# Six more half chunks of attention values as three float32r products, in an attention and mixture-of-experts kernel on one core

## The chip, the core and the metric

The kernel runs on one core of a Trainium2 chip. The core has TensorE (PE, with its weight loads shown as PEld), VectorE (DVE), ScalarE (ACT), GpSimd (POOL) and SyncE (SP), and 16 DMA engines. The metric is the device time of one execution in microseconds, the median of three runs.

## What is computed

```python
def _attn_ref(q, k, v, tau):                      # B, N, C = 4, 5056, 256
    qn = q / (np.linalg.norm(q, axis=1, keepdims=True) + 1e-06)
    kn = k / (np.linalg.norm(k, axis=1, keepdims=True) + 1e-06)
    s = kn.transpose(0, 2, 1) @ qn / tau          # 256 x 256 for each batch
    a = softmax(s, axis=-1)
    return v @ a                                  # 4 x 5056 x 256

def _moe_ref(x, w_gate, w1, w2):                  # 20224 tokens, 8 experts, F = 1024
    logits = x @ w_gate
    # greedy: largest logits first, each token to one expert, 2528 tokens to an expert
    for e in range(E):
        h = np.maximum(x[mask] @ w1[e], 0.0)
        out[mask] = h @ w2[e]
```

All inputs and the output are float32.

## The kernel before

**Stages.** First the scores of the four batches are made from q and k, with as much of the other work as fits beside the loads. Then comes the stage that the change touches, called the value stage here: the product v @ a for the batches 1 to 3 (what is left of it), whose rows are stored to x_d in HBM, while VectorE finds the tokens of expert 0 (route 0). Then the eight experts follow, each with five chunks of 512 tokens: tokens are gathered from x_d by indirect transfers (L1284), layer 1 (L1498) and layer 2 (L1549) run on TensorE, and the rows of the output are scattered (L1567). The routes of the experts 1 to 7 run on VectorE beside the layers of the experts before.

**The value stage.** The rows of v are tiled in chunks of 1024 rows, five to a batch, and a chunk in two halves of four tiles of 128 rows. A half chunk is done in one of two ways. *Plain* (x_tiles, L267): eight float32 matmuls, two for each tile. *Cloven* (x_tiles_cut, L583): v and a are each split in a high half (rounded to float32r) and a low half (what is left), and each float32 product becomes three float32r products, high by high, high by low and low by high: 24 matmuls. The string TURNS gives the order, F for a plain half chunk and C for a cloven one; before there are 12 F and 10 C, and eight plain pairs of tiles (four half chunks) follow. Both ways put two tiles in one PSUM tile px, which ScalarE copies to xs (L271, L587); a store to x_d of each half chunk is issued from ScalarE's queue (L277).

**The split of a half chunk** is done by cleave(): ScalarE writes minus the rounded values to the low part (L568), a transfer issued by GpSimd adds the raw values from HBM to it (L569, an accumulating transfer of 512 KB), and ScalarE writes the rounded values to the high part (L571). The split halves live in buffers named by PLACES (ub0, ub1, ua0 to ua2, vr); BEHIND says after how many F and C turns a buffer may be taken again.

**Route 0** is a search in eight rounds. A round is: VectorE compares (ge, L730), TensorE counts (20 small matmuls into the bank pc, L695, then one with Ex, L708), VectorE reads the counts (mxs, L715) and ScalarE copies them out of the bank (eq, L723). There is one bank pc: the counting of the next round writes it again and has to wait for the copy of the round before. Two lists of tokens are then made (L915 and L935 on TensorE, L953 on ScalarE, L969 on VectorE), the first with the four tiles of the first gather.

**What sets the order.** Each engine works its instructions in the order in which the program lists them. That order is made by a planner (class Order): tick() adds what TensorE does to the planner's time o.pe, and hook() puts VectorE's and ScalarE's pieces of the streams where the planner's time for them has come. advance() decides in the same way about the tokens of a chunk to come: if they landed early enough by the planner's time (`left(*todo[0]) > MOVE_LAT + 4000`), stage() flips them by VectorE and two DMAs by way of HBM (via, xT); if not, turn() transposes them on TensorE with eight matmuls (L1451), four at a time.

```python
        if todo and todo[0] not in BY_PE and landed.get(todo[0], 1e12) <= o.pe and left(*todo[0]) > MOVE_LAT + 4000:
            stage(*todo[0], 0)
            staging.append([todo[0], 1, 0, 1e12])
```

**The weights of expert 0** are loaded when its number is known (L1243) and split in eight pieces by split_piece() (ScalarE L1262, VectorE L1265), one piece after a pair of tiles or half a cloven half chunk; FREED says after how many C turns the buffers ua0 and ua1 are free for that. Layer 1 of expert 0 needs the first four pieces and the transposed tokens of its first chunk (xH by ScalarE, xL by VectorE).

Of the kernel before, what the change touches and what calls it, by code (L numbers as in the profile page):

```python
# [21 lines left out]
E, F = 8, 1024  # L22
# [84 lines left out]
def attention_moe(ctx: ExitStack, tc: tile.TileContext, q, k, vt, tau, wg, w1t, w2t, tabs, out):  # L107
# [449 lines left out]

    cloven = [(b, c, h) for b, c in CLOVEN for h in range(0, T, TH)]
    v_cut = []

    def cleave():
        b, c, h = cloven[len(v_cut)]
        home = PLACES[len(v_cut)]
        y = (vp.tile([128, 2048], F32, name="vr", bufs=BUFS_V) if home == "vr" else
             ffw.tile([128, 2048], F32, name=home)).bitcast(F32R)
# [5 lines left out]
        S.activation(y[:, 0], raw, AF.Copy)  # L571
        v_cut.append(y.rearrange("p z k (t n) -> p z k t n", t=TH))

    def x_tiles_cut(k, t, xs, tick):
        b = cloven[k][0]
# [1011 lines left out]
    with tc.manual_schedule():  # L1587
# [4 lines left out]
        def first_w():  # L1592
            load_w(0, 0)
            load_w(0, 1)
            cut_w[0] = [o.pe + LOAD_LAT] + list(SPLIT)
# [4 lines left out]
        def tend():  # L1600
            settle()
            if cut_w[0] and o.pe > cut_w[0][0] and len(cut_w[0]) > 1 and past.count("C") >= FREED[cut_w[0][1][0]]:
                split_piece(0, *cut_w[0].pop(1))
# [12 lines left out]
        place = halve_a(2)  # L1616
        for _ in range(3):
            cleave()
        place()
        P.memset(ge[:, :, NT:J], 0.0)  # L1620
        for kind in TURNS:
            while len(v_cut) < len(cloven) and len(v_cut) <= len(past) + 1:
                want_ = BEHIND.get(len(v_cut), "")
                if any(past.count(x) < want_.count(x) for x in set(want_)):
# [5 lines left out]
            else:  # L1630
                k = past.count("C")
                b, c, h = cloven[k]
# [9 lines left out]
        actx.close()  # L1642
        px_at[1] = False
# [159 lines left out]
```

## Time and profile before

| | us |
|---|---|
| median of three runs | 1211.24 (1211.0 to 1211.59) |
| time of the profiled execution | 1216.66 |
| its span, first to last instruction | 1214.6 |
| value stage in it, TensorE's first L267 of batch 3 to the first L1498 | 219.6 to 314.3 |

| engine | busy us of the span | share |
|---|---|---|
| PE | 1192.0 | 98% |
| PEld | 1069.0 | 88% |
| DVE | 893.6 | 74% |
| ACT | 579.6 | 48% |
| POOL | 411.2 | 34% |

The granted clock of TensorE is 0.998 of full speed over the span. Matmuls are pipelined, so the end of one row and the start of the next overlap; what a row of matmuls takes is read from its start to the start of the next row. A float32 matmul of the program stands as two in the trace's counts.

### The profile page before, as it was taken

The numbers are of one execution on the slowest core, as the hardware profiler recorded it, in microseconds if no ns is written. First come the engines' busy times: TensorE is split into PE (matmuls) and PEld (weight loads), VectorE is DVE, ScalarE is ACT, GpSimd is POOL, SyncE is SP. The second block draws the span as 40 slices with busy tenths as digits, with TensorE's granted clock in tenths as the row PEclk, the third lists the DMA queues.
The fourth block names the chain that finished last, engine by engine and source line by source line (L and its number), as shares of the span: only waits on it lengthen the run. The fifth ranks groups of instructions, "written<-read, shape, count | busy, mean of one in ns | idle before, by whom it ended". The sixth has DMA issues, their size and how long they took to land.

```text
span 1214.6 us, 22477 instructions
## 1 busy us (share of the span) xinstructions
PE 1192.0 (98%) x8201; PEld 1069.0 (88%) x8201; DVE 893.6 (74%) x2497; ACT 579.6 (48%) x1316; POOL 411.2 (34%) x659
## 2 busy tenths in 40 slices
PE   7999999999999999999999999999999999999998
PEld 6889877798889889999998999988888898898897
DVE  7788686778788888989888888798786555555541
ACT  6666644655343444444354454354445644344431
POOL 1000001110342543354434444444444444444422
PEclk9999999999999999999999999999999999999999
DMA  8998996785322413313422243243234233433310
GB/s 311 361 393 313 365 357 214 182 236 219 107 70 90 146 58 110 140 56 114 143 87 83 79 151 114 83 143 121 82 118 152 87 116 122 140 102 98 105 66 34
DMA packets 70542, 184.27 MB, mean 152 GB/s; under 512 B 11168, under 2 KB 34592, under 8 KB 65824
## 3 DMA queue, kind: packets, MB, share of 16 engines
q1 hardware_dynamic: 39808, 97.54, 22.4%
q0 software_dynamic: 20656, 63.72, 17.4%
q10 hardware_dynamic: 9968, 21.59, 4.6%
q8 instruction: 64, 1.05, 0.4%
q14 instruction: 46, 0.38, 0.1%
HBM read 123.04 MB, written 59.51 MB: 150 GB/s over the span
## 4 chain that ended last, share of the span: by engine, by line
PE 82%; DVE 7%; issue 5%; POOL 2%; DMA 2%; ACT 1%; SPq 0%; POOLq 0%; DVEq 0%; ACTq 0%
PE py L1549 30%; PE ph L1498 30%; PE s L345 8%; PE px L267 5%; PE pc L695 3%; PE px L583 2%; PE px L308 2%; PE px L461 1%; POOL out_dram L1567 1%; DMA ua<-in_q_dram 1%; DVE acc_q L355 1%; DVE hL L1507 1%; DVE acc_k L355 1%; DVE nf L412 1%; PE pi L935 1%
## 5 line engine op out<-in xcount | busy, mean ns | idle before, releaser
L1549 PE MATMUL py<-ua,hH 128*128 128x256 f32 (+2 forms) x1928 | 432.0, 312 | 0.0
L1498 PE MATMUL ph<-xH,ua 128*128 128x512 f32 (+1 forms) x1280 | 392.4, 380 | 1.2 <-DVE hL L1507 1.0
L1549 PE MATMUL py<-ua,hL 128*128 128x256 f32 (+1 forms) x1280 | 339.0, 275 | 0.0
L1549 PEld LDWEIGHTS py<-ua,hH 128*128 128x128 f32 (+1 forms) x1928 | 311.9, 190 | 14.0
L1502 ACT ACTIVATE hH<-ph 128x512 fp32r<-128x512 f32 (+1 forms) x320 | 189.8, 593 | 199.6 <-PE ph L1498 188.3
L1498 PEld LDWEIGHTS ph<-xH,ua 128*128 128x128 f32 x1280 | 240.8, 189 | 32.5 <-DVE hL L1507 2.9
L1507 DVE SCALAR_TENSOR_TENSOR hL<-ph,hH 128x512 fp32r<-128x512 f32 (+1 forms) x320 | 216.1, 677 | 58.8 <-ACT hH L1502 48.0
L1567 POOL DMA_INDIRECT out_dram<-y,idx x160 | 165.6, 1035 | 264.2 <-DVE y L1565 115.3
L1549 PEld LDWEIGHTS py<-ua,hL 128*128 128x128 f32 (+1 forms) x1280 | 243.4, 190 | 4.2
L1498 PE MATMUL ph<-xL,ua 128*128 128x512 f32 (+1 forms) x640 | 242.2, 378 | 0.2 <-DVE xL L1457 0.2
L1284 POOL DMA_INDIRECT xg<-x_d,src x160 | 164.0, 1025 | 91.0 <-issue 54.8
L1561 ACT ACTIVATE y<-py 128x256 f32<-128x256 f32 (+1 forms) x160 | 61.5, 384 | 251.4 <-PE py L1549 191.3
L345 PE MATMUL s<-ua 128*128 128x256 f32 (+1 forms) x640 | 144.4, 384 | 6.4 <-DMA ua<-in_q_dram 6.4
L345 PEld LDWEIGHTS s<-ua 128*128 128x128 f32 (+1 forms) x640 | 121.1, 192 | 26.1 <-DMA ua<-in_q_dram 6.4
L1498 PEld LDWEIGHTS ph<-xL,ua 128*128 128x128 f32 x640 | 121.1, 189 | 14.3 <-DVE xL L1457 0.8
L1565 DVE TENSOR_TENSOR y<-py,y 128x256 f32<-128x256 f32 x79 | 33.4, 423 | 98.3 <-ACT y L1561 95.6
L354 ACT ACTIVATE sq<-ua 128x1024 f32<-128x1024 f32 (+1 forms) x80 | 76.6, 970 | 54.3 <-DMA ua<-in_k_dram 18.2
L1295 POOL COPY spacer<-hH 1x1 f32<-1x1 f32 x114 | 26.1, 229 | 180.9 <-ACT hH L1502 173.0
L375 POOL TENSOR_SCALAR ny<-ny 128x4 f32<-128x4 f32 x4 | 2.0, 506 | 181.1 <-ACT ny L374 181.1
L1383 DVE TENSOR_TENSOR xL<-xT,xH 128x256 fp32r<-128x256 f32 x136 | 51.9, 426 | 6.1 <-ACT xH L1379 6.1
L1379 ACT ACTIVATE xH<-xT 128x256 fp32r<-128x256 f32 x136 | 54.1, 458 | 4.8 <-DMA xT<-via 4.8
L355 DVE TENSOR_TENSOR acc_k<-acc_k,sq 128x1024 f32<-128x1024 f32 (+2 forms) x40 | 44.3, 1113 | 11.2 <-ACT sq L354 10.4
(343 smaller groups left out, 1468.0 us busy)
## 6 DMA issues: line engine op xcount, KB each, us to landing
x_d<-xs ACTq DMA_DIRECT2D x40, 512.0 KB
ua<-in_k_dram SPq DMA_DIRECT2D x35, 512.0 KB
ua<-in_q_dram SPq DMA_DIRECT2D x35, 512.0 KB
via<-xs SPq DMA_DIRECT2D x34, 512.0 KB
xT<-via SPq DMA_DIRECT2D x136, 128.0 KB
vr<-in_vt_dram SPq DMA_DIRECT2D x14, 1024.0 KB
ua<-in_vt_dram SPq DMA_DIRECT2D x4, 1024.0 KB
ua<-in_vt_dram POOLq DMA_DIRECT2D x5, 512.0 KB
```

The source lines that it names most:

```text
L267: mm = PE.matmul(px[:, i * C:i * C + width], lhsT=vs[b, c][:, kb, t + i, :], rhs=a_f[b][:, kb, 0:width], start=(kb == 0), stop=(kb == 1))
L345: newest[0] = PE.matmul(sb[:, ib * C:(ib + 1) * C], lhsT=kt[:np_, t, ib * 128:(ib + 1) * 128], rhs=qt[:np_, t, :], start=(first and t == 0 ...
L354: S.activation(sq[:n, t0:t1], t_[:n, t0:t1], AF.Square)
L355: V.tensor_tensor(acc[:n, t0:t1], acc[:n, t0:t1], sq[:n, t0:t1], op=OP.add)
L1284: P.indirect_dma_start(out=xg[:n, i, :], out_offset=None, in_=rows, in_offset=bass.IndirectOffsetOnAxis(ap=routed[p]["src", col][:n, col:c ...
L1379: S.activation(hi[:, a], rows[:, a], AF.Copy)
L1498: PE.matmul(ph[:, 0:nt], lhsT=l[:, w], rhs=in_turn(x_, kb, nt).rearrange("p a m -> p m a"), start=(i == 0), stop=(i == 5))
L1502: S.activation(hH[:, fb, 0:nt], ph[:, 0:nt], AF.Relu)
L1507: V.scalar_tensor_tensor(hL[:, fb, 0:nt], ph[:, 0:nt], 0.0, hH[:, fb, 0:nt].bitcast(F32), op0=OP.max, op1=OP.subtract)
L1549: PE.matmul(to, lhsT=l[:, fb, tk], rhs=r, start=(fb == 0 and k_ == 0), stop=(fb == 7 and at_end), skip_group_check=twice)
L1561: S.activation(y[:n], py[:n, C:2 * C] if twice else one, AF.Copy)
L1567: sd = P.indirect_dma_start(out=out, out_offset=bass.IndirectOffsetOnAxis(ap=routed[p]["idx", col][:n, col:col + 1], axis=0), in_=y[:n], i ...
```

## The change

Six half chunks of batch 1 go from the plain to the cloven way: CLOVEN now names 16 half chunks, PLAIN five chunks, and TURNS has 6 F and 16 C. The eight plain pairs at the end remain. The a of batch 1 is split by halve_a_1() (two copies by ScalarE, one subtraction by VectorE). Three of the six half chunks (BY_DVE) get their low half by one subtraction on VectorE in place of ScalarE's first copy and the transfer; the other three as before. So there are 13 accumulating transfers of 512 KB in place of 10. One more buffer (own) is added, the rules for taking a buffer again are renewed (AFTER), cleave() may run one turn further ahead, and the weights of expert 0 are split only after all 16 C turns.

```diff
-PLAIN = ((3, 0), (1, 2), (3, 1), (3, 2), (1, 3), (1, 4), (3, 3), (3, 4))
-CLOVEN = ((2, 4), (2, 0), (2, 1), (2, 2), (2, 3))
-TURNS = "FFCFCFCFCFCFCFCFCFFCFC"
-PLACES = ("ub0", "ub1", "ua0", "ua1", "ub0", "ub1", "vr", "ua0", "ua1", "ua2")
-BEHIND = {3: "FF", 4: "C", 5: "CC", 6: "FFFF", 7: "CCC", 8: "CCCC", 9: "FFFFFF"}
-FREED = (9, 10)
+PLAIN = ((3, 0), (3, 1), (3, 2), (3, 3), (3, 4))
+CLOVEN = ((2, 4, 0), (1, 2, 0), (2, 4, 4), (2, 0, 0), (1, 2, 4), (2, 0, 4), (2, 1, 0), (1, 3, 0), (2, 1, 4), (2, 2, 0), (1, 3, 4),
+          (2, 2, 4), (2, 3, 0), (1, 4, 0), (2, 3, 4), (1, 4, 4))
+BY_DVE = (1, 4, 7)
+TURNS = "FFCCFCCCCFCCCCFCCCFCCC"
+PLACES = ("ub0", "ub1", "own", "ua0", "ua1", "ub0", "ub1", "own", "ua0", "ua1", "vr", "ub0", "own", "ua0", "vr", "ua1")
+AFTER = {4: (2, 0), 5: (0, 1), 6: (0, 2), 7: (0, 3), 8: (0, 4), 9: (0, 5), 11: (0, 6), 12: (0, 8), 13: (0, 9), 15: (0, 10)}
+FREED = 16
...
+    def halve_a_1():
+        a = a_f[1][:, :, 0:C].rearrange("p k (m a) -> p k m a", a=2)
+        h = apart(apool.tile([128, 2, GW], F32R, name="a0"))[:, :, :, 0:128]
+        S.activation(h.rearrange("p a k m -> p k m a"), a, AF.Copy)
+
+        def low():
+            less = x_rows()[:, 0:2].rearrange("p k (m a) -> p k m a", a=2)
+            V.tensor_tensor(less, a, h.rearrange("p a k m -> p k m a").bitcast(F32), op=OP.subtract)
+            lo = apart(apool.tile([128, 2, GW], F32R, name="a1"))[:, :, :, 0:128]
+            S.activation(lo.rearrange("p a k m -> p k m a"), less, AF.Copy)
+            a_two[1] = [h, lo]
...
-        S.activation(y[:, 1], raw, AF.Copy, scale=-1.0)
-        P.dma_start(out=y[:, 1], in_=vt[b, c].rearrange("p (k n) -> p k n", k=2)[:, :, h * 128:(h + TH) * 128],
-                    accum_op=OP.add)
+        if k_ not in BY_DVE:
+            S.activation(y[:, 1], raw, AF.Copy, scale=-1.0)
+            P.dma_start(out=y[:, 1], in_=vt[b, c].rearrange("p (k n) -> p k n", k=2)[:, :, h * 128:(h + TH) * 128],
+                        accum_op=OP.add)
         S.activation(y[:, 0], raw, AF.Copy)
+        if k_ in BY_DVE:
+            unit[0] += 1
+            o.post(o.pe + CUT_LAT, 1150,
+                   lambda: V.tensor_tensor(y[:, 1], raw, y[:, 0].bitcast(F32), op=OP.subtract), unit[0])
...
-            while len(v_cut) < len(cloven) and len(v_cut) <= len(past) + 1:
-                want_ = BEHIND.get(len(v_cut), "")
-                if any(past.count(x) < want_.count(x) for x in set(want_)):
+            while len(v_cut) < len(CLOVEN) and len(v_cut) <= len(past) + 2:
+                f_, c_ = AFTER.get(len(v_cut), (0, 0))
+                if past.count("F") < f_ or past.count("C") < c_:
                     break
                 cleave()
```

The lines of the changed kernel are shifted: L270 and L274 are the plain matmul and its copy, L612 and L616 the cloven ones, L590, L591 and L593 the copy, transfer and copy of cleave(), L724 and L737 the counting, L752 the copy of the counts, L1480 the transposes, L1527 and L1578 the two layers.

**ScalarE in the value stage, before.** From the copy of the counts of the second round (eq<-pc) to that of the third; xs<-px are the copies of the products, ua and vr the split halves.

```order
L723 ACTIVATE eq<-pc 128x120
L587 ACTIVATE xs<-px 128x512 x2
L277 DMA x_d<-xs 128x1024
L568 ACTIVATE ua_2085<-vr 128x1024
L571 ACTIVATE ua_2085<-vr 128x1024
L271 ACTIVATE xs<-px 128x512
L723 ACTIVATE eq<-pc 128x120
```

Between the two copies of counts stands one split. **The same place in the change**, again from the copy of the counts of the second round to that of the third:

```order
L752 ACTIVATE eq<-pc 128x120
L616 ACTIVATE xs<-px 128x512
L280 DMA x_d<-xs 128x1024
L590 ACTIVATE ua_2140<-vr 128x1024
L593 ACTIVATE ua_2140<-vr 128x1024
L590 ACTIVATE vr<-vr 128x1024
L593 ACTIVATE vr<-vr 128x1024
L616 ACTIVATE xs<-px 128x512 x2
L280 DMA x_d<-xs 128x1024
L590 ACTIVATE ub_2210<-vr 128x1024
L593 ACTIVATE ub_2210<-vr 128x1024
L752 ACTIVATE eq<-pc 128x120
```

Now three splits (six copies of 128x1024) and three copies of products stand ahead of the copy of the counts.

**TensorE at the same place, before**, from the third round's count with Ex (L708) to the next use of the bank pc (the small matmuls with ge, L695, 20 of them):

```order
L267 MATMUL px<-a_last,ua_1571 128x256 x3
L708 MATMUL pc<-Ex,ones_q 128x128
L267 MATMUL px<-a_last,ua_1571 128x256 x3
L583 MATMUL px<-a_two,ua_1851 128x256 x14
L695 LDWEIGHTS ge
L695 MATMUL pc<-oh,ge 128x64
```

**And in the change:**

```order
L612 MATMUL px<-a_two,ub_1897 128x256 x7
L270 MATMUL px<-a_last,ua_1571 128x256
L737 MATMUL pc<-Ex,ones_q 128x128
L270 MATMUL px<-a_last,ua_1571 128x256 x7
L724 LDWEIGHTS ge
L724 MATMUL pc<-oh,ge 128x64
```

The cloven half chunk ub_1897 is the one during which ScalarE is at the splits shown above; the 17 matmuls of it ahead of these rows have the 20 small matmuls of the third round behind them.

**TensorE in layer 2 of expert 0's fourth chunk, in the change**, where the first chunk of expert 1 is transposed:

```order
L1578 MATMUL py<-ua_3060,hH 128x256
L1578 MATMUL py<-ua_3059,hL 128x256
L1480 MATMUL pt<-identr,xg 128x128 x4
L1578 MATMUL py<-ua_3059,hH 128x256
L1578 MATMUL py<-ua_3060,hH 128x256
```

Before, no transposes stand here: this chunk goes by way of HBM. Over the program TensorE has 72 transposes in place of 48; the first chunk of expert 1, the second of expert 2 and the first of expert 3 are new among them, and SyncE's queue has 31 transfers to via in place of 34, and 124 from it in place of 136.

## Rows read from the trace of the kernel before

**Rows 1.** The page, busy time, share of the span and instructions.

```profile
PE 1192.0 (98%) x8201; PEld 1069.0 (88%) x8201; DVE 893.6 (74%) x2497; ACT 579.6 (48%) x1316; POOL 411.2 (34%) x659
```

**Rows 2.** Windows of the value stage: us, then busy us (instructions) by engine.

```profile
219.60:297.50 77.90, 77.14 (x626) 70.76 (x625) 65.04 (x227) 43.63 (x81) 9.91 (x10) 1.00 0.76 222
297.50:314.30 16.80, 15.58 (x96) 13.39 (x95) 13.50 (x45) 10.63 (x30) 4.34 (x4) 1.00 0.43 158
```

**Rows 3.** Timeline of TensorE: start, length, line, out<-in, count, idle before.

```profile
219.62 7.17 PE L267 MATMUL px<-a_last,ua 128*128 128x256 f32 x32
226.44 3.03 PE L583 MATMUL px<-a_two,ub 128*128 128x256 f32 x24
...
240.68 0.23 PE L708 MATMUL pc<-Ex,ones_q 128*128 128x128 f32 x1
240.74 2.56 PE L583 MATMUL px<-a_two,ua 128*128 128x256 f32 x21
243.14 1.03 PE L267 MATMUL px<-a_last,ua 128*128 128x256 f32 x4
244.00 0.75 PE L695 MATMUL pc<-oh,ge 128*128 128x64 bf16 x20
244.59 1.54 PE L267 MATMUL px<-a_last,ua 128*128 128x256 f32 x6
...
281.80 0.44 PE L935 MATMUL pi<-E__97,G 128*128 128x162 bf16 x4
...
290.84 0.59 PE L935 MATMUL pi<-E__97,G 128*128 128x162 bf16 x6
291.27 0.64 PE L267 MATMUL px<-a,vr 128*128 128x256 f32 x2
...
297.54 5.34 PE L267 MATMUL px<-a_last,vr 128*128 128x256 f32 x24
...
309.46 0.62 PE L1451 MATMUL pt<-identr,xg 128*128 128x128 f32 x2 [1.16 <-DMA xg<-x_d,src]
```

**Rows 4.** Timeline of TensorE in layer 2 of expert 0, around four transposes.

```profile
334.52 0.39 PE L1549 MATMUL py<-ua,hH 128*128 128x256 f32 x2
...
334.85 0.39 PE L1549 MATMUL py<-ua,hH 128*128 128x256 f32 x2
...
335.19 0.45 PE L1451 MATMUL pt<-identr,xg 128*128 128x128 f32 x4
...
335.88 0.39 PE L1549 MATMUL py<-ua,hH 128*128 128x256 f32 x2
```

**Rows 5.** Timeline of ScalarE in the value stage.

```profile
243.46 0.25 ACT L723 ACTIVATE eq<-pc 128x120 f32<-128x120 f32 x1
243.61 1.07 ACT L587 ACTIVATE xs<-px 128x512 f32<-128x512 f32 x2
244.72 0.33 ACTq L277 DMA_DIRECT2D x_d<-xs  x1
245.09 1.06 ACT L568 ACTIVATE ua<-vr 128x1024 fp32r<-128x1024 f32 x1 [0.40 <-ACT xs L587]
...
247.00 0.58 ACT L271 ACTIVATE xs<-px 128x512 f32<-128x512 f32 x1
...
298.15 0.60 ACT L587 ACTIVATE xs<-px 128x512 f32<-128x512 f32 x1
```

**Rows 6.** Timeline of GpSimd: two issues of accumulating transfers, and the first gather.

```profile
238.94 1.09 POOL L569 DMA_DIRECT2D ub<-in_vt_dram  x1 [5.28 <-ACT ub L568]
...
302.40 0.95 POOL L1284 DMA_INDIRECT xg<-x_d,src  x1 [20.91 <-ACT xs L271]
```

**Rows 7.** DMA from 245 to 265 us: busy tenths of 40 slices of 0.5 us.

```profile
DMA  8689999999899999999989999999997999999999
```

**Rows 8.** Timeline of VectorE: the end of the first list, and a subtraction of 128x512.

```profile
285.74 0.16 DVE L1010 SCALAR_TENSOR_TENSOR src<-k,w__2659 128x4 int32<-128x4 int32 x1
...
313.04 0.69 DVE L1457 TENSOR_TENSOR xL<-pt,xH 128x512 fp32r<-128x512 f32 x1 [1.30 <-ACT xH L1454]
```

**Rows 9.** Groups by line and form: a two-operand pass of 128x1024 on VectorE, mean ns.

```profile
L355 DVE TENSOR_TENSOR acc_q<-acc_q,sq 128x1024 f32<-128x1024 f32 x32 | 39.1, 1221 | 2.5 <-ACT sq L354 2.3
```

More of the change, by code (lines that the diff above doesn't have):

```diff
@@ L69 @@
 HOMES = {(1, 0): "ub", (1, 1): "ub", (2, 4): "ua", (3, 0): "ua", (3, 1): "ua", (3, 2): "ua", (3, 3): "late", (3, 4): "late"}
-PLAIN = ((3, 0), (1, 2), (3, 1), (3, 2), (1, 3), (1, 4), (3, 3), (3, 4))
-CLOVEN = ((2, 4), (2, 0), (2, 1), (2, 2), (2, 3))
-TURNS = "FFCFCFCFCFCFCFCFCFFCFC"
-PLACES = ("ub0", "ub1", "ua0", "ua1", "ub0", "ub1", "vr", "ua0", "ua1", "ua2")
-BEHIND = {3: "FF", 4: "C", 5: "CC", 6: "FFFF", 7: "CCC", 8: "CCCC", 9: "FFFFFF"}
-FREED = (9, 10)
+PLAIN = ((3, 0), (3, 1), (3, 2), (3, 3), (3, 4))
[6 more added lines that the diff above has]
+FREED = 16
+CUT_LAT = 3000
 CUT = (4, 4, 4, 4, 4)
@@ L556, in halve_a @@
         return place
-    cloven = [(b, c, h) for b, c in CLOVEN for h in range(0, T, TH)]
+    def halve_a_1():
[9 more added lines that the diff above has]
+        unit[0] += 1
+        o.post(o.pe + CUT_LAT, 600, low, unit[0])
+    cctx = ExitStack()
+    own = cctx.enter_context(tc.tile_pool(name="own", bufs=1))
     v_cut = []
+    lows_of = {}
     def cleave():
-        b, c, h = cloven[len(v_cut)]
-        home = PLACES[len(v_cut)]
-        y = (vp.tile([128, 2048], F32, name="vr", bufs=BUFS_V) if home == "vr" else
+        k_ = len(v_cut)
+        b, c, h = CLOVEN[k_]
+        home = PLACES[k_]
+        y = (own.tile([128, 2048], F32, name="own") if home == "own" else
+             vp.tile([128, 2048], F32, name="vr", bufs=BUFS_V) if home == "vr" else
              ffw.tile([128, 2048], F32, name=home)).bitcast(F32R)
@@ L567, in cleave @@
         raw = vs[b, c][:, :, h:h + TH].rearrange("p k t n -> p k (t n)")
-        S.activation(y[:, 1], raw, AF.Copy, scale=-1.0)
-        P.dma_start(out=y[:, 1], in_=vt[b, c].rearrange("p (k n) -> p k n", k=2)[:, :, h * 128:(h + TH) * 128],
-                    accum_op=OP.add)
+        if k_ not in BY_DVE:
+            S.activation(y[:, 1], raw, AF.Copy, scale=-1.0)
+            P.dma_start(out=y[:, 1], in_=vt[b, c].rearrange("p (k n) -> p k n", k=2)[:, :, h * 128:(h + TH) * 128],
+                        accum_op=OP.add)
         S.activation(y[:, 0], raw, AF.Copy)
+        if k_ in BY_DVE:
+            unit[0] += 1
+            o.post(o.pe + CUT_LAT, 1150,
+                   lambda: V.tensor_tensor(y[:, 1], raw, y[:, 0].bitcast(F32), op=OP.subtract), unit[0])
+        lows_of[k_] = unit[0]
         v_cut.append(y.rearrange("p z k (t n) -> p z k t n", t=TH))
     def x_tiles_cut(k, t, xs, tick):
-        b = cloven[k][0]
+        b = CLOVEN[k][0]
+        if b == 1:
+            o.flush(lows_of[k])
         px = next_px()
@@ L1592, in first_w @@
         def first_w():
+            assert past.count("C") >= 12
             load_w(0, 0)
@@ L1601, in tend @@
             settle()
-            if cut_w[0] and o.pe > cut_w[0][0] and len(cut_w[0]) > 1 and past.count("C") >= FREED[cut_w[0][1][0]]:
+            if cut_w[0] and o.pe > cut_w[0][0] and len(cut_w[0]) > 1 and past.count("C") >= FREED:
                 split_piece(0, *cut_w[0].pop(1))
@@ L1616, in attention_moe @@
         place = halve_a(2)
+        halve_a_1()
         for _ in range(3):
@@ L1631, in attention_moe @@
                 k = past.count("C")
-                b, c, h = cloven[k]
+                b, c, h = CLOVEN[k]
                 xs = x_rows()
@@ L1642, in attention_moe @@
         actx.close()
+        cctx.close()
         px_at[1] = False
```

## The prediction

> **What bounds the kernel now.** I read the busy times first [rows 1]: TensorE is busy in 1192.0 of 1214.6 us, 98%, the next engine, VectorE, in 74%. So a change counts here by what it takes from TensorE's work and by the waits that it makes on TensorE. Then the windows of the value stage [rows 2]: TensorE is busy in 77.14 of 77.9 us and 15.58 of 16.8 us, so there are only about 2 us of idle time in the stage, 1.16 us of them in one wait, for the first gathered tokens at 309.46 [rows 3]. VectorE is busy in 65.0 of the 77.9 us and ScalarE in 43.6; neither bounds the stage by its sum, but both work in the order listed, and TensorE can wait for a single copy that stands behind others. Third, the timelines, for the prices and the places.
>
> **TensorE's work in the six half chunks.** Two plain half chunks run from 219.62 to 226.44 [rows 3], 3.41 us each, or 0.426 us for each of eight matmuls. Of a cloven half chunk 21 matmuls run from 240.74 to 243.14, 0.114 us each, so 24 take 2.74 us. Six half chunks save 6 x 0.67 = **4.0 us**, all of it on the path, because TensorE is busy throughout.
>
> **TensorE's work that comes back.** The order shows 72 transposes on TensorE in place of 48: three chunks of experts 1 to 3 no longer reach the planner's limit for the way by HBM, because the routes of the experts now fall later against the layers. Their price is in layer 2 of expert 0 [rows 4]: a group of three matmuls follows the one before by 0.33 us (334.52 to 334.85); the two groups around four transposes take 1.03 us (334.85 to 335.88) in place of 0.68. So four transposes cost 0.35 us, and the six new fours **2.1 us**. I take the same price where they stand in layer 1. Nothing hides them, since TensorE has no idle time there. What they free on VectorE, SyncE and the DMA queues was not waited for.
>
> **New waits for ScalarE.** The bank pc is counted into again only after ScalarE has copied the last counts. Before, that copy ran from 243.46 to 243.71 [rows 5], and the next count began at 244.00 [rows 3]: 0.3 us to spare, with one split between the copies of counts. In the change three splits stand between the second and the third. Prices on ScalarE [rows 5]: a split 1.91 us (245.09 to 247.00), a copy of a product 0.5 (two in 1.07), a store's issue 0.37 (244.72 to 245.09), the copy of counts 0.25; a product is complete 0.16 us after the next one's first matmul (240.74 + 2.56 against 243.14 [rows 3]). From the start of the cloven half chunk ub_1897, ScalarE needs 0.16 + 0.5 + 0.37 + 2 x 1.91 + 2 x 0.5 + 0.37 + 1.91 + 0.25 = 8.4 us until the counts are copied. TensorE comes to the next count after 24 x 0.114 + 0.59 for the 20 small matmuls (244.00 to 244.59) + 8 x 0.426 + 0.06 = 6.8 us. It waits **1.6 us**. The same addition for the next place with two splits in a row (the copy of counts of the sixth round, behind ua_2427 and vr), begun one half chunk earlier because ScalarE is then already late, gives 9.1 us against 8.3: **0.9 us**. Elsewhere one split lies between copies, as before. Together 2.5 us. The bounds are 0 (if the copies overlap more than these rows show) and 2.5; I take 2.5, because the same rows show only 0.3 us to spare with one split, and two more cost 3.8.
>
> **The wait for the first gather.** It is 1.16 us before. The gathers start when the last cloven half chunk's store has landed: that half chunk ends at 297.54, its last copy starts at 298.15, behind work on the lists, and the first gather at 302.40 [rows 3, 5, 6]. In the change no such work stands ahead of that copy, so it can start 0.16 us after the end, 0.45 us earlier. And the second list's small matmuls now lie between that point and the transposes, 14 in place of 1; six take 0.43 us (290.84 to 291.27), so TensorE arrives 0.9 us later. Together 1.3 us, so the wait goes: **-1.2 us** (bound: 0).
>
> **VectorE.** It gets one subtraction of 128x512 (0.69 us [rows 8]) and three of 128x1024, which the trace does not show in this form; the nearest row is a two-operand pass of 128x1024 at 1.22 us [rows 9]. That is 4.4 us in a stage with 12.9 us idle, and the search may end as much later. Its cover: the first list needs 3.9 us from its tests at 281.80 to 285.74 [rows 3, 8], and before lies 16.7 us ahead of the gather. In the change 53 cloven matmuls (6.1 us) lie between the tests and the last half chunk's end, and 4.9 us more up to the gather: 7 us of cover remain. If that went, each us would be a us on TensorE. In the last stretch all eight weight subtractions now stand (before, two were done ahead of 297.5), with the second list and the start of route 1; the second four transposes wait for VectorE to empty their bank. Bounds 0 and 1.4 us, two subtractions of 0.69; VectorE had 3.3 us idle there [rows 2], so I take **0.4 us**.
>
> **The transfers.** Three more on queues that were busy from 245 to 265 us without a break [rows 7]. Their cover is the lead: the shortest is from the issue after the fourth cloven half chunk to its use after four more, one plain one and two counts, 15.6 us less 2.7 us for the copies ahead of the issue: 12.9 us. Six transfers issued from 238.94 on [rows 6] were through by 265 us, 4.3 us each with the stores beside them. So I count nothing.
>
> **The sum.** -4.0 + 2.1 + 2.5 - 1.2 + 0.4 = -0.2 us. The profiled execution took 1216.66 us, so it would be 1216.5; it lies 5.4 us above the median of the runs, 1211.24, and against that median the forecast is **1211.0 us**, no change that a measurement can tell (0.2% are 2.4 us). The later routes may cost or spare some tenths in the experts, counted at nothing: their first gathers have several us of TensorE's work ahead of them.
>
> **Rival 1, faster: only TensorE's work counts.** If ScalarE's copies do not hold the counts and VectorE is not late, the sum is -4.0 + 2.1 - 1.2 = -3.1 us: 1208.1 us. For it: ScalarE is busy in only 56% of the stage [rows 2]. Against it: the addition above, and 0.3 us to spare. The Trainium skill, "Perfetto Trace Analysis", section "Identifying the Most-Contended Engine", says that kernels gain by working on the engine with the highest occupancy first. By that rule ScalarE at half occupancy would be no concern and this rival would be the forecast; the trace agrees in that TensorE is at 98%, but it has no room between the two copies. Chance 0.16.
>
> **Rival 2, slower: the accumulating transfers land late.** Four are issued close together, for the ninth to the twelfth cloven half chunk; the last of them is needed about 28 us after the fourth cloven half chunk's end (7 x 2.74 + 2 x 3.41 + four counts of 0.6), 25.7 us after the first issue. So the place decides against the change when a transfer takes over 6.4 us; at 7.4 us each the fourth is 4 us late, and the time is -0.2 + 4.0 = +3.8 us: 1215.0 us. For it: the queues were full with fewer [rows 7], and runs of four cloven half chunks make stores follow each other faster, too. Against it: 4.3 us for each under the same load. Chance 0.15.
>
> **Rival 3: the transposes are free.** If they fall into waits for VectorE that exist anyway, 2.1 us less: -2.3 us, 1208.9 us, still no change that can be told. Chance 0.07.
>
> **How the numbers follow.** The forecast has 0.62, rival 3 0.07, rival 1 0.16, rival 2 0.15. The first two lie within 0.2% (0.69 together), rival 1 is faster (0.16), rival 2 slower (0.15). The range goes from rival 1's 1208.1, rounded to 1208.0, to 1213.6: the forecast with the gather's wait kept and VectorE's bound (-4.0 + 2.1 + 2.5 + 1.4 = +2.0 us), and a little of rival 2.
>
> **What would show it.** Right: TensorE's plain matmuls down by a third in the stage, the stage some 2 to 3 us shorter, 72 transposes, and about 2 us more in the experts; two waits of TensorE for ScalarE ahead of the small matmuls with ge, 1.6 and 0.9 us; none for the first gather. Rival 1: no such waits. Rival 2: TensorE's first matmul of a cloven half chunk waits for a DMA. Wrong altogether: an end of the stage that is not earlier, or waits of several us in the experts 1 to 3.

## The result, and the profile after

The changed kernel takes 1217.38 us (median of eight runs, 1214.2 to 1219.16); the kernel before, run beside it, 1210.61 us. The ratio is 1.0054, 95% interval 1.0039 to 1.0070: slower by 6.8 us (4.7 to 8.5). The prediction, 1211.0 us and no change, was wrong, and its range ended at 1213.6 us.

The profiled execution took 1218.52 us (span 1216.7). The kernel before took 1209.6 us beside runs 1 to 4 below, 1216.4 beside 5 to 7, 1219.1 beside 8 and 9 and 1215.4 beside 10 and 11, so between these groups only ratios are compared. Its profiled execution of 1216.66 us lies among the later groups, the changed kernel's was taken beside 1210.6 us. The value stage takes the same in a second execution (94.67 and 94.57 us before, 97.25 and 97.24 after, runs 4 and 2 in the table below) and can be compared in us. What lies ahead of it and behind it varies more: the same instructions of TensorE bring seven traces of the changed kernel and its relatives to the stage at 217.89 to 222.41 us, and the kernel before took 1207.6 to 1213.5 us in the 23 executions beside runs 1 to 4. So what is read of the experts from two single traces is uncertain by some us; it is compared with run 4.

Busy times of the changed kernel [rows 1], its two windows of the stage [rows 2], and three windows of 4 us behind (columns: us, then busy us (instructions) of PE, PEld, DVE, ACT, POOL, then TensorE's granted clock, the DMA share and GB/s):

```profile
PE 1190.5 (98%) x8273; PEld 1071.5 (88%) x8273; DVE 894.7 (74%) x2489; ACT 589.5 (48%) x1321; POOL 415.8 (34%) x655
```

```profile
219.60:297.50 77.90, 75.11 (x683) 69.64 (x672) 62.65 (x208) 53.60 (x86) 15.35 (x15) 1.00 0.90 246
297.50:314.30 16.80, 12.63 (x64) 10.48 (x63) 11.77 (x33) 10.18 (x29) 5.76 (x4) 0.88 0.51 180
...
308.00:312.00 4.00, 0.56 (x2) 0.28 (x2) 0.05 (x1) 0.43 (x1) 0.35 (x1) 0.80 0.55 173
312.00:316.00 4.00, 3.96 (x13) 3.26 (x13) 2.44 (x9) 1.42 (x6) 0.00 (x0) 0.50 0.00 0
316.00:320.00 4.00, 4.00 (x20) 3.45 (x19) 2.45 (x4) 3.50 (x9) 0.00 (x0) 0.85 0.00 0
```

TensorE does less work, and what is left of the span is idle time at the end of the stage, with a granted clock of 0.50, that is 1.2 GHz, behind it. The DMA share of the long window went from 0.76 to 0.90. TensorE's timeline, changed kernel [rows 3]:

```profile
221.26 7.17 PE L270 MATMUL px<-a_last,ua 128*128 128x256 f32 x32
228.08 3.03 PE L612 MATMUL px<-a_two,ub 128*128 128x256 f32 x24
...
255.85 0.74 PE L724 MATMUL pc<-oh,ge 128*128 128x64 bf16 x20 [1.75 <-ACT eq L752]
...
272.01 0.74 PE L724 MATMUL pc<-oh,ge 128*128 128x64 bf16 x20 [0.68 <-ACT eq L752]
...
289.63 2.84 PE L612 MATMUL px<-a_two,vr 128*128 128x256 f32 x24
292.31 2.84 PE L612 MATMUL px<-a,ua 128*128 128x256 f32 x24
294.99 1.03 PE L270 MATMUL px<-a_last,vr 128*128 128x256 f32 x4
296.29 0.16 PE L944 MATMUL pc<-cb,before 128*128 128x1 bf16 x1 [0.27 <-DVE cb L938]
...
306.90 0.41 PE L1480 MATMUL pt<-identr,xg 128*128 128x128 f32 x1
308.45 0.64 PE L1480 MATMUL pt<-identr,xg 128*128 128x128 f32 x2 [1.14 <-DMA xg<-x_d,src]
312.04 0.37 PE L1480 MATMUL pt<-identr,xg 128*128 128x128 f32 x1 [2.95 <-DMA xg<-x_d,src]
312.20 0.63 PE L964 MATMUL pi<-E__97,G 128*128 128x162 bf16 x3
312.63 3.69 PE L270 MATMUL px<-a_last,vr 128*128 128x256 f32 x8
315.76 1.03 PE L1480 MATMUL pt<-identr,xg 128*128 128x128 f32 x4
316.59 2.27 PE L270 MATMUL px<-a_last,vr 128*128 128x256 f32 x8
318.51 0.57 PE L1527 MATMUL ph<-xH,ua 128*128 128x512 f32 x1
```

The stage, 221.26 to 318.51, is 97.25 us; before it was 94.67. The two waits for ScalarE's copy of counts are where they were expected, 1.75 and 0.68 us. The wait for the first gather did not go: it is 1.14 + 2.95 = 4.09 us in place of 1.16. And behind it everything is slow: eight matmuls in the trace's counts take 3.13 us (312.63 to 315.76), where the eight before took 1.61 (309.92 to 311.53, rows below); three list matmuls 0.43 in place of 0.21, four transposes 0.83 in place of 0.48, the next eight matmuls 1.92 in place of 1.69. That is 2.3 us for the clock alone. The kernel before at the same place:

```profile
309.92 1.96 PE L267 MATMUL px<-a_last,vr 128*128 128x256 f32 x8
311.53 0.64 PE L1451 MATMUL pt<-identr,xg 128*128 128x128 f32 x4
```

Why the gather is late stands on GpSimd and on ScalarE's queue. First the kernel before, then the changed one; L1243 and L1272 are the two weight loads of expert 0, L277 and L280 the issue of the store behind the last cloven half chunk, L1284 and L1313 the first of four gathers [rows 5, 6]:

```profile
279.12 1.09 POOL L1243 DMA_INDIRECT ub<-in_w1t_dram,ei  x1 [21.18 <-PE px L583]
280.51 0.98 POOL L1243 DMA_INDIRECT ub<-in_w2t_dram,ei  x1 [0.31 <-issue]
...
298.79 0.33 ACTq L277 DMA_DIRECT2D x_d<-xs  x1
```

```profile
286.70 1.09 POOL L1272 DMA_INDIRECT ub<-in_w1t_dram,ei  x1 [11.41 <-PE px L270]
288.09 0.98 POOL L1272 DMA_INDIRECT ub<-in_w2t_dram,ei  x1 [0.31 <-issue]
...
295.82 0.33 ACTq L280 DMA_DIRECT2D x_d<-xs  x1
...
301.68 1.71 POOL L1313 DMA_INDIRECT xg<-x_d,src  x1 [12.61 <-ACT junk L982]
```

The loads, 2 MB, now go out 7.6 us later (5.9 us later counted from the start of the stage), 8 us ahead of the last cloven half chunk's end, while three cloven half chunks in a row store 512 KB every 2.7 us. From the store's issue to the first gather it is 5.9 us (295.82 to 301.68) in place of 3.6 (298.79 to 302.40). The view of that one store (KB, then us from issue to landing) in the changed kernel:

```profile
x_d<-xs ACTq DMA_DIRECT2D x1, 512.0 KB, 4.7
```

It lands at 300.50; before, by the landing times in the trace, it took 2.6 us (301.40). The gather follows 1.2 and 1.0 us behind the landing. The list of its tokens was ready at 293.8 us, so it is the store that the gather waits for. The queues show the pile, windows of the kernel before first, then of the changed one:

```profile
292.00:296.00 4.00, 3.95 (x29) 3.50 (x28) 3.83 (x16) 3.05 (x9) 0.00 (x0) 1.00 0.20 81
296.00:300.00 4.00, 4.00 (x28) 3.72 (x27) 3.45 (x8) 3.60 (x12) 0.00 (x0) 1.00 0.43 172
```

```profile
292.00:296.00 4.00, 4.00 (x33) 3.67 (x32) 3.69 (x21) 1.79 (x3) 0.00 (x0) 1.00 1.02 423
296.00:300.00 4.00, 3.69 (x23) 3.17 (x22) 3.79 (x14) 1.72 (x4) 0.00 (x0) 1.00 0.92 378
```

From the first gather to the transpose of the fourth tile it is 10.4 us (312.04) in place of 7.4 (309.80, the second matmul of the row at 309.46), 3.0 us more. The loads do not stand beside the gathers: by the landing times they were through at 294.1 and 297.9 us, ahead of the first gather. What is longer is GpSimd's issue of the four, 5.4 us from the first to the fourth in place of 4.3, and the way of the fourth, 4.9 us from issue to landing in place of 3.1. Its rows, before and after:

```profile
306.71 0.94 POOL L1284 DMA_INDIRECT xg<-x_d,src  x1 [0.30 <-issue]
...
307.09 1.26 POOL L1313 DMA_INDIRECT xg<-x_d,src  x1 [0.30 <-issue]
```

Why is open (last section).

### The profile page after: what moved, and what is told of

Its sections match the earlier page's. It is cut to its first block, busy times and chain, and to the rows that moved or that the text cites. A ratio compares the mean times of both kernels' runs of the same rounds, so it can differ in the third digit from the quotient of the medians.

```text
span 1216.7 us, 22576 instructions
## 1 busy us (share of the span) xinstructions
PE 1190.5 (98%) x8273; PEld 1071.5 (88%) x8273; DVE 894.7 (74%) x2489; ACT 589.5 (48%) x1321; POOL 415.8 (34%) x655
## 3 DMA queue, kind: packets, MB, share of 16 engines
q8 instruction: 65, 1.06, 0.4%
## 4 chain that ended last, share of the span: by engine, by line
PE 73%; DVE 8%; issue 7%; DMA 5%; ACT 4%; POOL 3%; ACTq 0%; POOLq 0%; SPq 0%; DVEq 0%
PE ph L1527 28%; PE py L1578 27%; PE s L348 7%; PE pc L724 2%; PE px L270 2%; DMA ua<-in_q_dram 2%; POOL out_dram L1596 2%; PE px L311 1%; PE px L612 1%; PE px L464 1%; DMA x_d<-xs 1%; DVE hL L1536 1%; POOL xg L1313 1%; ACT xs L616 1%; DMA xg<-x_d,src 1%
## 5 line engine op out<-in xcount | busy, mean ns | idle before, releaser
L1578 PE MATMUL py<-ua,hH 128*128 128x256 f32 (+2 forms) x1928 | 431.9, 312 | 0.0
L1527 PE MATMUL ph<-xH,ua 128*128 128x512 f32 (+1 forms) x1280 | 390.6, 379 | 0.0
L1578 PE MATMUL py<-ua,hL 128*128 128x256 f32 (+1 forms) x1280 | 338.9, 275 | 0.0
L1578 PEld LDWEIGHTS py<-ua,hH 128*128 128x128 f32 (+1 forms) x1928 | 311.6, 190 | 13.9
L1527 PEld LDWEIGHTS ph<-xH,ua 128*128 128x128 f32 x1280 | 240.5, 189 | 29.7 <-DVE hL L1536 0.6
L1578 PEld LDWEIGHTS py<-ua,hL 128*128 128x128 f32 (+1 forms) x1280 | 243.2, 190 | 4.2
L1527 PE MATMUL ph<-xL,ua 128*128 128x512 f32 (+1 forms) x640 | 242.6, 379 | 0.1
L1313 POOL DMA_INDIRECT xg<-x_d,src x160 | 165.6, 1035 | 86.2 <-issue 52.6
L1527 PEld LDWEIGHTS ph<-xL,ua 128*128 128x128 f32 x640 | 121.1, 189 | 14.4 <-DVE xL L1486 0.5
L1324 POOL COPY spacer<-hH 1x1 f32<-1x1 f32 x107 | 23.5, 220 | 148.4 <-ACT hH L1531 141.3
L1412 DVE TENSOR_TENSOR xL<-xT,xH 128x256 fp32r<-128x256 f32 x124 | 47.7, 429 | 8.8 <-ACT xH L1408 8.6
L1408 ACT ACTIVATE xH<-xT 128x256 fp32r<-128x256 f32 x124 | 49.6, 460 | 6.6 <-DMA xT<-via 6.5
```

What stands on the lines that cost most here:

```text
L1313: P.indirect_dma_start(out=xg[:n, i, :], out_offset=None, in_=rows, in_offset=bass.IndirectOffsetOnAxis(ap=routed[p]["src", col][:n, col:c ...
L1408: S.activation(hi[:, a], rows[:, a], AF.Copy)
L1412: V.tensor_tensor(lo[:, a], rows[:, a], hi[:, a].bitcast(F32), op=OP.subtract)
L1527: PE.matmul(ph[:, 0:nt], lhsT=l[:, w], rhs=in_turn(x_, kb, nt).rearrange("p a m -> p m a"), start=(i == 0), stop=(i == 5))
L1578: PE.matmul(to, lhsT=l[:, fb, tk], rhs=r, start=(fb == 0 and k_ == 0), stop=(fb == 7 and at_end), skip_group_check=twice)
```

## The experiments

The theories: **A**, the weight loads' new place delays the last store and the gathers, and the clock falls in the wait; **B**, the stores alone follow each other too closely; and for the rest of the loss, the transposes, ScalarE's copies, and VectorE in the experts. "Stage" is always TensorE's first plain matmul of batch 3 to the first of layer 1.

| run | ratio to before | stage, us | wait for first gather | clock behind it | transposes |
|---|---|---|---|---|---|
| before | 1 | 94.67 | 1.16 | 1.00 | 48 |
| the change | 1.0054 (1.0039 to 1.0070) | 97.25 | 4.09 | 0.50 | 72 |
| 1, second load later | 1.0067 (1.0051 to 1.0083) | 90.95 | 0.67 | 1.00 | 72 |
| 2, limit lowered | 1.0086 (1.0069 to 1.0104) | 97.24 | 3.87 | 0.50 | 56 |
| 3, lead of one | 1.0027 (1.0018 to 1.0036) | 95.08 | 3.84 | 0.50 | 72 |
| 4, before, 72 transposes | 1.0016 (1.0003 to 1.0029) | 94.57 | 1.06 | 1.00 | 72 |
| 5, filled wait | 1.0032 (1.0020 to 1.0045) | 95.61 | 0.53 | 1.00 | 72 |
| 6, before, loads listed later | 0.9986 (0.9974 to 0.9997) | 97.36 | 2.29 | 0.50 | 48 |
| 7, three edits | 0.9987 (0.9976 to 0.9999) | 89.13 | 0.91 | 1.00 | 64 |
| 8, before, loads held | 0.9990 (0.9978 to 1.0002) | 96.07 | 2.26 | 1.00 | 48 |
| 9, all by transfers | 1.0064 (1.0045 to 1.0084) | 95.31 | 2.78 | 0.50 | 56 |
| 10, all by VectorE | 0.9967 (0.9955 to 0.9978) | 89.16 | 1.03 | 1.00 | 72 |
| 11, four by VectorE | 1.0001 (0.9990 to 1.0011) | 89.23 | 1.23 | 1.00 | 64 |

**Run 1.** The second weight load behind the gathers (and BY_PE with (2,1) and (3,0), which keeps the 72 transposes):

```diff
             load_w(0, 0)
-            load_w(0, 1)
-            cut_w[0] = [o.pe + LOAD_LAT] + list(SPLIT)
+            cut_w[0] = [o.pe + LOAD_LAT] + list(SPLIT[0:4])
...
                 while queue:
                     gather()
+                load_w(0, 1)
...
-h[0] = layer1(p, 0, {} if p == 0 else ...
+h[0] = layer1(p, 0, {at: [lambda q_=q_: split_piece(0, 1, q_, None)] for q_, at in enumerate((4, 5, 6, 7))} if p == 0 else ...
```

> The changed kernel, with the load of expert 0's second weight matrix (1 MB) issued behind the first chunk's four gathers instead of ahead of them, its four pieces split beside layer 1 of the first chunk; 72 transposes as in the changed kernel. Theory A (the two weight loads, issued 8 us later than before, share the queues with the last stores to x_d, so that the first gathers start and land late, and the clock falls in that wait): one of the two loads less means 1 MB, some 3 us at the 400 GB/s of that stretch; the first gather starts by 299.5 to 300 us in place of 301.7, the wait for it falls from 4.1 us to about 1, the granted clock stays at 1.00, and the time falls by 3 to 5 us against the changed kernel (1212.4 to 1214.4). Theory B (the last three cloven half chunks store too close together for the queue, the loads do not matter): wait and clock as in the changed kernel, 1217.4 us. Theory C (the wait is of no account, the time went elsewhere): the wait goes but the time stays within 1 us of the changed kernel.

Timeline of ScalarE's queue, GpSimd, TensorE and VectorE in run 1: the store behind the last cloven half chunk, the first gather, the wait for it, and a place in the experts:

```profile
292.51 0.33 ACTq L280 DMA_DIRECT2D x_d<-xs  x1
...
296.31 1.10 POOL L1313 DMA_INDIRECT xg<-x_d,src  x1 [11.76 <-PE pi L964]
...
304.82 0.28 PE L1480 MATMUL pt<-identr,xg 128*128 128x128 f32 x1 [0.67 <-DMA xg<-x_d,src]
...
607.57 0.71 DVE L1376 STREAM_TRANSPOSE xs<-xg 128x512 f32<-128x512 f32 x1 [2.92 <-DMA out_dram<-y,idx]
608.92 0.48 PE L1527 MATMUL ph<-xH,ua 128*128 128x512 f32 x1 [2.23 <-DVE hL L1536]
```

3.8 us from the store's issue to the gather (the store landed after 2.6 us, as before the change), a wait of 0.67, clock 1.00, and a stage 6.3 us shorter than the changed kernel's. A holds in the stage and B falls: the stores are as close as in the changed kernel. Not all of the 6.3 us need be the load's: the edit also takes four of the eight weight splits out of the last stretch, and from the first gather to the fourth tile's transpose it is now 8.5 us. And the time did not move. The rest behind the stage grew from 898.2 to 903.0 us in the profiled execution, the fastest of the six: VectorE stood for 2.92 us in front of a transposition (L1376) that waited for a DMA, hL was queued behind it, TensorE waited 2.23 us for hL, and its granted clock was 0.50 from 610 to 613 us. By the medians the rest grew by nearly 8 us; the trace does not show where the others lost more. Of theory C this much is right: a stage that is shorter by 6 us is not a kernel that is.

**Run 2.** `MOVE_LAT + 4000` becomes `MOVE_LAT`.

> The changed kernel with the planner's limit for the way by HBM lowered from MOVE_LAT + 4000 to MOVE_LAT: 56 transposes on TensorE in place of 72 (the second chunk of expert 2 and the first of expert 3 go by HBM again, the first of expert 1 does not). By the prediction's price of 0.35 us for four, 1.4 us less than the changed kernel, 1216.0 us; by rival 3 (the transposes are free) 1217.4; if the way by HBM now comes too late for its chunks, waits of TensorE for xH or xL ahead of layer 1 and more than 1217.4. The stage ahead of the experts is the same as in the changed kernel, and its waits (two for eq of 1.8 and 0.7, the first gather 4.1 us, clock below 1.00 for some 5 us) should show again if they belong to the program.

Slower than the change by 0.32%, 3.9 us: the third case. The stage is the same to 0.01 us, so its waits belong to the program. In the experts TensorE waits 2.2 us for xH and 0.5 for xL of the chunks that came by HBM, the worst pair at 655.25 and 656.24 us with the clock at 0.50 from 658 to 660. A lower limit does not pay here: the transposes are the cheaper way for routes this late. Other limits were not tried.

**Run 3.** `len(v_cut) <= len(past) + 2` becomes `+ 1`.

> The changed kernel with cleave() one turn less ahead, as before the change. Two splits in place of three then stand ahead of ScalarE's third copy of counts, while the second place with two splits in a row stays. If the waits for that copy are what three splits in a row cost: the wait of 1.75 us goes to below 0.3, that of 0.7 stays, and the time falls by 1.5 us, to 1215.9. If the accumulating transfers have no lead to spare (rival 2): a cloven matmul waits for a DMA, and nothing is gained or the time grows. If the first gather's wait takes up what is won (the gathers start by their own clock): the wait there grows by as much and the time stays at 1217.4.

The wait of 1.75 us is gone (the third count starts with no wait at 253.73), the one of 0.69 stays, the stage is 2.2 us shorter and the ratio down by 0.27% (3.3 us). No cloven matmul waits for a DMA, so the lead was longer than it had to be.

**Run 4.** BY_PE gets (1,0), (2,1), (3,0) and (3,1), in the kernel before.

> The kernel before, with the four chunks (1,0), (2,1), (3,0) and (3,1) always transposed on TensorE: 72 transposes in place of 48, and no other difference in the value stage. By the prediction's price 2.1 us more than before: 1212.7 us. By rival 3 no difference: 1210.6. Its stage is that of before and shows how much of the 1.16 us wait for the first gather, and of the waits for Ex in the experts, comes back in a second execution.

0.16% is 2.0 us (0.4 to 3.5): the prediction's 2.1. The experts take 895.7 us here, and 898.2 in the changed kernel with as many transposes, so by these two traces 2.5 us of the loss are left for them. By the medians it is less: 0.38%, 4.6 us, lie between the two kernels, and 2.7 of them in the stage. The groups of TensorE's instructions behind the stage say where (busy us, mean ns | idle before them), kernel before, then changed:

```profile
L695 PE MATMUL pc<-oh,ge 128*128 128x48 bf16 (+3 forms) x940 | 32.2, 182 | 0.2 <-DVE ge L730 0.2
```

```profile
L724 PE MATMUL pc<-oh,ge 128*128 128x48 bf16 (+3 forms) x960 | 33.1, 182 | 0.4 <-DVE ge L759 0.3
```

And TensorE's timeline of the changed kernel in the experts:

```profile
427.12 0.28 PE L1480 MATMUL pt<-identr,xg 128*128 128x128 f32 x1 [0.90 <-DMA xg<-x_d,src]
...
723.34 0.30 PE L737 MATMUL pc<-Ex,ones_q 128*128 128x64 f32 x1 [1.23 <-DVE Ex L733]
```

One count of 20 matmuls (0.6 us) that stood in the stage before now stands in the experts, and there are waits of 0.90 and 1.23 us that run 4 does not have. Run 3 repeats both (0.87 and 1.25), and runs 2 and 5 the first (0.90 and 0.86), so that one belongs to the change. The waits for Ex come and go: the kernel before has five for TensorE's count with Ex in its own trace (3.7 us together), and run 4 none.

**Run 5.** Nine matmuls with no reader ahead of the first transposes:

```diff
+            if n == LATE - 2:
+                fill = next_px()
+                for i in range(9):
+                    PE.matmul(fill[:, 0:C], lhsT=vs[3, 4][:, 0, 0, :], rhs=a_f[3][:, 0, 0:C], start=True, stop=True)
```

> The changed kernel with nine more float32 matmuls of 128x256 (18 in the trace's counts, 3.8 us at full clock), whose result nobody reads, ahead of the first four transposes, where TensorE waits 4.1 us for the first gather. They only fill the wait: the gathers, stores and loads are as in the changed kernel. If the fall of the granted clock to 0.50 behind that wait is a cost of its own: the clock stays at 1.00, the wait is down to some 0.3 to 1 us, and the stage is 2.2 us shorter than the changed kernel's 97.25 us (the rows behind the wait: 1.4 us on eight matmuls, 0.35 on four transposes, 0.4 on the rest), some 95.0 us, the time 1215.2. If the clock falls for another reason, or its price is not that: stage 97.2 us, 1217.4.

The same windows as above, run 5:

```profile
308.00:312.00 4.00, 3.47 (x19) 2.92 (x17) 0.34 (x2) 0.48 (x1) 0.69 (x1) 1.00 0.59 189
312.00:316.00 4.00, 3.98 (x23) 3.30 (x24) 3.03 (x10) 3.20 (x10) 0.00 (x0) 1.00 0.00 0
```

With useless work in the wait the clock stays at 1.00. The stage is 1.6 us shorter, although the first wait for the counts was 2.10 us here, 0.35 longer; together 2.0 of the 2.2 expected. The ratio goes from 1.0054 to 1.0032, 2.7 us less.

**Runs 6 and 8.** Are late loads enough by themselves? Run 6 lists the loads behind the ninth cloven half chunk; run 8 makes GpSimd wait there as well (BY_PE with (3,1) keeps 48 transposes in both). The edit of run 8:

```diff
-        want(("ei", 0), first_w)
...
                     x_tiles_cut(k, t, xs, o.tick)
                     tend()
+                    if k == 8 and t == 0:
+                        P.tensor_copy(pace, xs[0:1, 0, 0:1])
+                        want(("ei", 0), first_w)
```

> The kernel before, with both weight loads of expert 0 issued behind the ninth of the ten cloven half chunks, about 10 us later than before and as close to the end of the last cloven half chunk as in the changed kernel (some 8 us ahead of it); 48 transposes. It asks whether the place of the loads alone delays the gathers, or only together with cloven half chunks that store every 2.7 us. Loads alone: the first gather starts 5 to 6 us after the last store's issue in place of 3.6, the wait for it grows from 1.1 to 3 us or more, and the granted clock falls; stage 97 us or more in place of 94.6. Together only: the stores come every 3.5 to 4.5 us here, so the queue is through with the loads in time, the gather starts within 4 us of the last store, the wait stays near 1.1 us and the stage at 94.6 us.

> The kernel before, with GpSimd held back by a one-element copy of the ninth cloven half chunk's first product ahead of expert 0's two weight loads, so that they are issued at about 288.5 us (9 us ahead of the last cloven half chunk's end, 8.3 in the changed kernel), and not at 279; 48 transposes. In the sixth run the loads were only listed later and still went out at 278.8 us, since GpSimd had nothing else to do, so the question stands. Late loads alone do it: the store of the last cloven half chunk lands more than 5 us after its issue, the four gathers end after 310.5 us in place of 309.4, TensorE waits 2 to 4 us in place of 1.1, the granted clock falls to 0.50 for some us and the stage grows from 94.6 to 97 us or more. Late loads only together with stores every 2.7 us: the first gather still starts 3.6 to 4 us after the last store's issue and the wait stays near 1.1 us, the stage at 94.6 to 95.

Run 6 missed its aim: GpSimd had nothing else to do and issued the loads at 278.79 us. That it waits 2.29 us all the same, with all eight weight splits moved into the last stretch, is not explained. Run 8, timeline of GpSimd, ScalarE's queue and TensorE:

```profile
291.22 1.34 POOL L1243 DMA_INDIRECT ub<-in_w1t_dram,ei  x1 [0.61 <-PE pc L915]
...
300.66 0.33 ACTq L277 DMA_DIRECT2D x_d<-xs  x1
...
305.39 0.96 POOL L1284 DMA_INDIRECT xg<-x_d,src  x1 [11.46 <-PE px L267]
...
312.55 0.28 PE L1451 MATMUL pt<-identr,xg 128*128 128x128 f32 x1 [1.86 <-DMA xg<-x_d,src]
313.23 0.28 PE L1451 MATMUL pt<-identr,xg 128*128 128x128 f32 x1 [0.40 <-DMA xg<-x_d,src]
```

Store to gather 4.7 us, between the 3.6 of before and the 5.9 of the change; the wait doubled; the stage is 1.4 us longer, 0.2 of them a count with Ex that stood behind the stage before. It lies between the two cases: late loads delay the gather even with stores 3.1 us or more apart, by about half of what they do together with the close ones. Run 6's wait shows that the splits' place may have a part in that, too; the two were not taken apart. And neither kernel is slower than the one before, although their stages are 2.7 and 1.4 us longer, with the clock at 0.50 again behind waits of 2.27 and 3.17 us for xL at 341.64 and 343.90: here, too, the stage is not the time.

**Run 7.** Runs 1 and 3 together, and the splits 14 and 15 one turn later each (AFTER 14: (0, 10), 15: (5, 10)).

> The changed kernel with the second weight load behind the first gathers (as in the first run), cleave() one turn less ahead (as in the third), and the last three splits each in a turn of its own in place of two together; the planner is left alone, which gives 64 transposes. By the sum of the parts: no wait for the copy of counts (-2.4 us), first gather waited for by less than 1 us and no fall of the clock (-5.5 us in the stage, 90.95 us measured with the first part alone): a stage of 88.5 us, 6 us shorter than before. The experts: 64 transposes, 1.4 us more than before. If they have no new waits, 4.5 us less than before, 1205.5 us; if they take back the gain as in the first run (a wait of 2.2 us for VectorE, with a fall of the clock behind it), 1209 to 1211.

**Run 9** is run 7 with BY_DVE = (), **run 10** with all six half chunks in it, **run 11** with four, (1, 4, 7, 10).

> The seventh run's kernel, with BY_DVE empty: all six added half chunks get their low half by the accumulating transfer, none by VectorE, so three more transfers of 512 KB and six fewer us of VectorE's and ScalarE's work together (3.6 less on VectorE, 3 x 0.95 more on ScalarE); 56 transposes. If the experts take the gain back because the routes on VectorE end later: the routes come 3 us earlier, the waits for VectorE and the eight transposes less give 1 to 3 us, and the ratio to before goes from 0.9987 to 0.996 to 0.998. If the transfers are at their limit (rival 2): cloven matmuls wait for a DMA, the first gather comes late again, the stage is longer than 90 us and the ratio 1.000 or more.

> The seventh run's kernel, with all six added half chunks' low halves made by VectorE (three more subtractions, 3.5 us on VectorE, and three transfers of 512 KB less, 10 in all as before the change); 72 transposes. It is the counterpart of the ninth run, which had six transfers more than before and was slower in the stage and behind it. If the queues are the tight resource of the stage: the first gather comes earlier against TensorE than in the seventh run, no wait for it, the stage 88 to 89.5 us; the experts pay eight more transposes (0.7 us), ratio 0.998 to 1.000. If VectorE is the tight resource: the lists and routes come 3.5 us later, TensorE waits for cb, src or Ex in the stage and behind it, ratio 1.001 to 1.004.

> The seventh run's kernel, with four of the six low halves by VectorE in place of three; 64 transposes as in the seventh run. Between the seventh and the tenth run: by the queues as the tight resource 0.997 to 0.9985, by VectorE as the tight resource 0.999 to 1.001.

Run 7's stage, 89.13 us, is near the sum (88.5), with one wait for the counts left, 0.36 us; of the 5.5 us that the stage has won on the kernel before, the time keeps 1.6, so the experts take most of it back, as in run 1. In the expectation of run 9, "six fewer us of VectorE's and ScalarE's work together" is a slip: VectorE has 3.6 us less and ScalarE 2.9 more. Run 9 bears out its second case, though no cloven matmul waits for a DMA: with one load out of the way the first gather still starts 5.7 us behind the last store's issue (298.34 to 304.04), the clock falls again, the counts wait 1.3 us for ScalarE, and TensorE 1.6 us for VectorE's tb and cb. Six accumulating transfers more than before are too many here, with ScalarE's copies that go with them; the two were not taken apart. A wait of 3.1 us for xL at 343 us, with a clock of 0.50 behind it, adds to run 9's time. Run 10 is the best kernel of all, 0.33% faster than before (0.22 to 0.45), with ten accumulating transfers as before and no wait for the copy of the counts. TensorE in it:

```profile
306.54 0.28 PE L1480 MATMUL pt<-identr,xg 128*128 128x128 f32 x1 [1.03 <-DMA xg<-x_d,src]
306.66 1.96 PE L270 MATMUL px<-a_last,vr 128*128 128x256 f32 x8
...
310.36 0.57 PE L1527 MATMUL ph<-xH,ua 128*128 128x512 f32 x1
```

But runs 7, 10 and 11 have stages within 0.1 us, so its gain lies in the experts (901.8 us against 904.8 and 904.6 behind the stage), and its wait for the first gather, 1.03 us, did not go as its first case has it. Run 11 does not lie between 7 and 10 as expected; its 1.0001 is in the range of the case in which VectorE is tight. What helps run 10 in the experts is open. That VectorE is the tight resource does not hold for the stage: the longest wait for it there is 0.24 us in run 10.

## Why the prediction was wrong

The sign that the prediction gave for being wrong altogether came true: an end of the stage that is not earlier (2.6 us later, counted from its start). Against its own steps:

- **TensorE's work, -4.0 us: right.** Two plain half chunks take 6.82 us (221.26 to 228.08), a cloven one 2.68 (289.63 to 292.31): six times 0.73 is 4.4.
- **Transposes, +2.1: right**, 2.0 (0.4 to 3.5) in run 4. Rival 3 falls, by an interval that ends not far from nothing.
- **Waits for ScalarE, +2.5: right**, 1.75 + 0.68 = 2.43, and run 3 removes the first by parting the splits. With it falls rival 1. The Trainium skill, "Perfetto Trace Analysis", section "Identifying the Most-Contended Engine", says to optimize the engine with the highest occupancy first. The trace shows what that leaves out: two waits of TensorE for one copy of ScalarE, which is busy in 69% of the long window (56% before).
- **"So the wait goes: -1.2": this step failed.** Its two halves came true. The last copy starts 0.20 us behind the half chunk's end (295.19), and TensorE arrives later, 11.9 us behind that end (294.99 to 306.90) in place of 10.3. But the step took the time from the copy to the gather, and from the gather to its tokens, from the kernel before, where the queues were at 0.20 and 0.43. It did not ask where expert 0's two loads had gone when the search and the last cloven half chunks drew together. They went in among the last stores: 2.3 us more from the store to the gather, which run 1 shows by taking one load away (0.2 us more). From the gather to the tokens it took 3.0 us more, and why that is stays open, since both loads had landed by then. Together the wait is 2.9 us longer than before. The bound given for this step was 0, so a longer wait stood nowhere in the sum.
- **Not in the sum at all: the clock.** 2.3 us by the rows, 1.6 to 2.0 by run 5.
- **VectorE, +0.4: not seen.** The wait for cb even fell, from 0.67 to 0.27; that was not forecast.
- **Transfers at nothing: right for the change** (no cloven matmul waits for a DMA, rival 2 falls), but with less room than it says. From 238.94 on the kernel before issues five accumulating transfers, not six, and the last lands at 265.8: 5.4 us each in place of 4.3, against the 6.4 at which the place would have decided. Run 9, with three more, was slower.
- **Later routes at nothing: wrong by about 2 us**, 2.5 by two traces and 1.9 by the medians, neither clear of noise by itself. TensorE waits 0.90 us for a gather, which four traces show (the change, runs 2, 3 and 5), and 0.6 us are the first count of route 1, which moved behind the stage; whether the 1.23 us for Ex are the change's is not shown.

The stage by these parts: -4.4 + 2.4 + 2.9 + 2.3 - 0.4 - 0.6 (the count that moved) = +2.2 us; measured +2.6. With 2.0 for the transposes and 2.5 for the rest of the experts, 2.6 makes 7.1 us, where the runs gave 6.8 (4.7 to 8.5). That it meets so well is partly luck, by the 2.5. Measured on the time and not on the stage, three parts are shown: the first wait for ScalarE (run 3, 3.3 us), the filled wait (run 5, 2.7) and the transposes (run 4, 2.0), each uncertain by 1.6 to 2.4 us. The late gather is shown in the stage alone, since run 1's time did not fall.

## What to carry over

When TensorE's work ahead of a fixed chain (search, list, store, gather) is cut, list every transfer that is triggered along that chain, and ask what each will now stand beside; a transfer on another queue is not out of the way. Price a wait of TensorE with the clock that follows it, and prefer an order in which some independent matmuls stand in front of a wait that may grow. And measure the whole kernel: in runs 1 and 7 the experts gave back most of what the stage had won, and in runs 6 and 8 a longer stage cost no time.

## What the runs showed of the hardware

The granted clock fell to 0.50 in or behind waits in which TensorE did next to nothing: 1.14 + 2.95 us in the change, 2.23 in run 1's experts, 2.29 in run 6, 1.30 + 1.48 in run 9, and came back some 3 to 7 us later, while TensorE was busy. It stayed at 1.00 behind 1.16 us in the kernel before and 1.86 + 0.40 in run 8. The Trainium skill, "TensorE: Matmul & The Clock Gate", section "What's actually happening", says that the array runs at half or full clock by how busy it has been lately; the trace agrees (0.50 and 1.00).

A store of 512 KB from ScalarE's queue held up its reader for 3.6 us with the DMA share at 0.43 (window 296 to 300 us) and for 5.9 behind two loads from GpSimd's queue, with the share at 0.92. The Trainium skill, "Trainium Kernel Development and Optimization", section "Key Constraints", says that transfers issued from several engines run on the same 16 DMA engines and interleave; run 1 agrees, 3.8 us with one load less.

Three of the four first gathers took GpSimd 1.71, 1.84 and 1.26 us in the change; before, three took 0.95 and one 1.49. Over the gathers of all thirteen traces it goes with VectorE: of 954 with no TENSOR_TENSOR of VectorE in their first 0.9 us, one took over 1.2 us; of 558 with 0.5 us or more of it, 134 did. No run tests this, and it does not explain why the fourth gather landed later.
